# Reordering the DMA transposes at the end of each phase, and spreading the loads of x, in a causal convolution followed by a multiplicative feed-forward layer

## The chip, the core and the metric

The kernel runs on one core of a Trainium2 chip. The metric is the device time of one execution in microseconds (us); the median of three runs of the kernel before is 564.67 us (563.21 to 564.77). A core has five engines with instruction streams of their own: TensorE (PE in the profile, with its weight loads as PEld), VectorE (DVE), ScalarE (ACT), GpSimd (POOL) and SyncE (SP). In this kernel SP does nothing but issue DMAs: every store, and every transpose that a DMA does. POOL issues the DMAs that convert float32 to bfloat16 on the way. "SPq" in a row is the issue of a DMA by SP, and such issues follow each other in program order.

## The reference

The input x has 8 sequences of 3904 tokens with 192 features. Each of 8 heads (24 features) has 7 taps; a softmax over the taps gives the weights of a causal convolution along the sequence. Its result goes through a gated product:

```python
w = softmax(weight)                              # 8 heads x 7 taps
out = np.einsum('hk,bskhg->bshg', w, x_unf)      # causal, 6 zero rows ahead of each sequence
a = x @ w1                                       # x: 31232 x 192, w1 and w2: 192 x 1024
b = x @ w2
h = a * b @ w3                                   # w3: 1024 x 1024
return h @ w_out                                 # w_out: 1024 x 192
```

There is no nonlinearity behind w3, so the kernel multiplies w3 and w_out once (`W_sb`, 1024 x 192) and computes (a*b) @ W_sb.

## The kernel before, in words

**Tiling.** The 31232 tokens are two halves of 15616 (`NS = 2`); both halves are worked on side by side. A half is cut into 31 rounds of 512 tokens (`CH`). For a round, `first_product` computes for 8 slices of 128 of the 1024 columns the products `pa` and `pb` on PE (six matmuls each), ACT copies `pa` to bfloat16 (`asb`), and DVE multiplies it by `pb` into `abT` (L495). `second_product` then multiplies `abT` by `W_sb` on PE (`ops`, 32 matmuls), ACT copies the result to `osb`, and SP stores it to the output. `pa`, `pb`, `ops` and the convolution's `cps` take turns in four tiles of PSUM, so a `pa` or `pb` can start only when ACT or DVE has read an older one.

**Phases.** The first three rounds are a prologue. After that the program is written out as phases 0 to 14. Phase 0 has no first product; phase p from 1 on has the first products of rounds 2p+1 and 2p+2, then one side convolution on DVE (phases 1 to 12), then four second products of two older rounds (`seconds`, n = 0 to 3), between which units of the convolution on PE are placed, and last the DMA transposes for later phases. The order of the lines is the order in which each engine, and SP's queue, gets its work.

**Two ways to convolve.** The first product needs the convolved x transposed, with features on the partitions.

- Most rounds go over PE. The windows of x (32 rows, 26 of them new) are loaded in blocks b (`x_jobs`, into `xb`, six buffers, one or two parts per block), multiplied by a band matrix in units of some heads (`convolve`, `conv`, 18 units in blocks 4 to 9; `places` says after which second product of which phase), copied to `convo` by ACT, and when a block's last unit is done, stored to a scratch tensor `rows` in DRAM by SP (`store`, L349 and L356). The rounds that the block completes are put on the list `due`. From `rows` a DMA transpose brings them to `xT` (`transposes`, L390: three DMAs a round). `xT` is a ring of four rounds. Block 4 completes rounds 5 and 6 (in phase 0), block 5 rounds 7 and 8 (phase 1), block 6 rounds 11 to 14 (phase 3), block 7 rounds 17 to 20 (phase 6), block 8 rounds 23 to 26 (phase 9), block 9 rounds 29 and 30 (phase 11).
- The rounds of phases 4, 7, 10 and 13 (`SIDE`) go over DVE. Three times each, once for every 64 features, x is copied by two DMAs of POOL to a scratch tensor in bfloat16 (`side_cast`, into `rows_c`), transposed by two DMAs of SP (`side_transpose`, L427, into `raw`, two buffers) and convolved on DVE by seven instructions or more (`side_conv`, L437 and L444, from `raw` over `acc` into `side`). The cast of a task is issued in phase p, its transpose at the end of phase p, and its convolution on DVE behind the first products of phase p+1.

**POOL.** In a phase with casts or loads to issue (`jobs`), POOL copies two elements of a freshly written `abT` (`pace`, L682) at set points of the first products (`points`: round of the phase and slice), and behind each copy issues an equal share of the DMAs. The copy only holds POOL back until DVE has got there. `zero_rows` are the windows that start a sequence; POOL clears six rows of them (L675).

The end of a phase, before the change:

```python
        while due:
            transposes(due.pop(0))
        if p + 1 in tasks:
            side_transpose(*tasks[p + 1])
```

Of the kernel before, what the change touches and what calls it, by code (L numbers as in the profile page):

```python
# [16 lines left out]
def kernel(  # L17
# [10 lines left out]
    nc = tc.nc  # L28
# [6 lines left out]
    PAD = K - 1  # L35
# [70 lines left out]
    def shape_of(b):  # L106
        n = SIZES[b] // 4
        m = n // (1 if b < 3 else 2)
        return n, m, n // m
# [4 lines left out]
    xb_of, zero_rows = {}, {}  # L114

    def group(r, e):
        return slice((2 * r + e) * C, (2 * r + e) * C + C)
# [13 lines left out]
    def x_jobs(b, part):  # L131
        js = parts_of(b)[part]
        n, m, E = shape_of(b)
        tiles = xb_of.setdefault(b, {})

        def alloc():
            xb = work.tile([128, XN], BF16, tag="xb", bufs=6, name="xb")
            xb = xb[:, 0:len(js) * m * D].rearrange("p (w d) -> p w d", d=D)
            for j in js:
                tiles[j] = (xb, (j - js[0]) * m)  # L140
                for e in range(E):
                    for u in range(m):
                        i = FIRST[b] + j * n + u * E + e
                        if tok(i) % S == 0 and i:
                            zero_rows.setdefault(b, []).extend(
                                (xb, group(r, e).start, tiles[j][1] + u) for r in range(NS))

        def job(first, r, e, s, t, w):
            def run():
                if first:  # L150
                    alloc()
                nc.gpsimd.dma_start(  # L152
                    out=tiles[js[0]][0][group(r, e), s:s + w, :],
                    in_=bass.AP(tensor=x.tensor, offset=(r * TS + t - PAD) * D,
                                ap=[[D, C], [E * ST * D, w], [1, D]]))
            return run

        todo = [(r, e, s, t, w) for e in range(E) for s, t, w in runs_of(b, js, e)
                for r in range(NS)]
        return [job(i == 0, *a) for i, a in enumerate(todo)]  # L160
# [12 lines left out]
    for r in range(NS):  # L173
        p = group(r, 0).start
# [98 lines left out]
    p = group(1, 0).start  # L273
# [112 lines left out]
    def transposes(R, first=0):  # L386
        t0, t1 = max(R * CH, first), min((R + 1) * CH, TS)
        a = ring_of[R] * CH % RING + t0 - R * CH
        for k in range(NP):
            nc.sync.dma_start_transpose(  # L390
                out=xT[k][:, a:a + t1 - t0], in_=rows[t0:t1, k * 128:(k + 1) * 128])
# [17 lines left out]
    def side_span(p):  # L409
        return (2 * p + 1) * CH, (2 * p + 3) * CH  # L410

    def side_cast(p, k):
        t0, t1 = side_span(p)

        def job(r):
            def run():
                nc.gpsimd.dma_start(  # L417
                    out=rows_c[t0 - HALO:t1, k, r * Q:r * Q + Q],
                    in_=x_rows[r * TS + t0 - HALO:r * TS + t1, k * Q:k * Q + Q])
            return run  # L420
        return [job(r) for r in range(NS)]

    def side_transpose(p, k):
        t0, t1 = side_span(p)
        raw_of[p, k] = stage.tile([128, HALO + 2 * CH], BF16, tag="w3T", bufs=2, name="raw")
        for lo, hi in ((t0 - HALO, t0 + CH), (t0 + CH, t1)):
            nc.sync.dma_start_transpose(  # L427
                out=raw_of[p, k][:, HALO + lo - t0:HALO + hi - t0], in_=rows_c[lo:hi, k, :])
# [42 lines left out]
    def first_product(R, between=None):  # L471
        N = width(R)
        ab = work.tile([128, JT, NS, CH], BF16, tag="abT", bufs=LAG + 1, name="abT")
        abT_of[R] = ab
        per = CH // N if CH % N == 0 else 1
        for f0 in range(0, JT, per):
            pq = []
            for i in range(2):
                p = banks("pa" if i == 0 else "pb")
                pq.append(p)  # L480
                for f in range(per):
                    ft = f0 + f
                    for k in range(NP):
                        for r in range(NS):
                            rs = slice(Q * r, Q * r + Q)
                            nc.tensor.matmul(  # L486
                                p[:, r, f * N:f * N + N],
                                w_of(i, k, r)[rs, ft * 128:(ft + 1) * 128],
                                operand(R, k, rs),
                                start=(k == 0), stop=(k == NP - 1))  # L490
            pa, pb = pq
            asb = work.tile([128, NS, CH], BF16, tag="asb", bufs=3, name="asb")
            nc.scalar.copy(out=asb[:, :, 0:per * N], in_=pa[:, :, 0:per * N])  # L493
            if per == 1:
                nc.vector.tensor_tensor(out=ab[:, f0, :, 0:N], in0=asb[:, :, 0:N],  # L495
                                        in1=pb[:, :, 0:N], op=ALU.mult)
            else:
                i0, i1 = (t.rearrange("p r (f n) -> p r f n", f=per) for t in (asb, pb))
                nc.vector.tensor_tensor(
                    out=ab[:, f0:f0 + per, :, 0:N].rearrange("p f r n -> p r f n"),  # L500
                    in0=i0, in1=i1, op=ALU.mult)
            if between and f0 in between:
                between[f0]()
# [110 lines left out]
    def later_loads():  # L614
# [6 lines left out]
        for f in side_cast(SIDE[0], 0):  # L621
# [24 lines left out]
    units = [(b, h, n) for b in range(4, NB)  # L646
             for n in [max(v for v in (2, 4) if v * shape_of(b)[1] * G <= CH)]
             for h in range(0, H, n)]
    places = {0: (0, 1), 1: (0, 2), 2: (0, 2), 3: (0, 2), 4: (0,), 5: (0,), 6: (0, 2), 7: (0,),
              8: (0,), 9: (0, 2), 10: (0,), 11: (0,)}  # L650
    assert sum(map(len, places.values())) == len(units)
    tasks = {q - NP + k: (q, k) for q in SIDE for k in range(NP)}
    jobs = {p: side_cast(*tasks[p + 1]) for p in range(1, len(phases)) if p + 1 in tasks}
    for p, b, part in ((1, 6, 0), (1, 6, 1), (2, 7, 0), (3, 7, 1), (5, 8, 0), (6, 8, 1), (8, 9, 0)):
        jobs[p] = jobs.get(p, []) + x_jobs(b, part)
    points = ((0, 1), (0, 4), (0, 7), (1, 2), (1, 5))
    sent = [LAG + 3]
    due = []

    def convolve(p):  # L660
        b, h, n = units.pop(0)
        conv(b, h * G, n * G, (V, A) if p not in tasks else (A, A))
        if h + n == H:
            store(b)
            while sent[0] < len(conv_rounds) and \
                    min((conv_rounds[sent[0]] + 1) * CH, TS) <= spans[b - 3][1]:
                due.append(conv_rounds[sent[0]])
                sent[0] += 1
# [1 line left out]
    pace = const.tile([1, 2], BF16)  # L670
    done = 0
    for p, rounds in enumerate(phases):
        for b in {u[0] for u in units[:3]}:
            for xb, p0, w in zero_rows.pop(b, []):
                nc.gpsimd.memset(xb[p0:p0 + PAD, w, :], 0.0)  # L675
        if p == 1:
            P(out=wC[Q:128], in_=wC[0:Q])
        todo = jobs.pop(p, [])

        def issue(R, ft, n):  # L680
            def run():
                P(out=pace, in_=abT_of[R][0:1, ft, 1, 0:2])  # L682
                for _ in range(min(n, len(todo))):
                    todo.pop(0)()
            return run

        each = -(-len(todo) // len(points))
        for j, R in enumerate(rounds):
            first_product(R, {ft: issue(R, ft, each) for a, ft in points if a == j and todo})
        assert not todo  # L690
        if p in tasks:
            side_conv(*tasks[p])
        last = NR if p == len(phases) - 1 else done + 2
        seconds = [(R, r) for R in range(done, last) for r in range(NS)]
        done = last
        for n, (R, r) in enumerate(seconds):
            (last_product if (R, r) == (NR - 1, NS - 1) else second_product)(R, r)
            if n in places.get(p, ()):
                convolve(p)
        while due:  # L700
            transposes(due.pop(0))
        if p + 1 in tasks:
            side_transpose(*tasks[p + 1])
    assert not units and not due and not jobs and done == NR and sent[0] == len(conv_rounds)


# [28 lines left out]
```

## Time and profile before

| | |
|---|---|
| median of the runs | 564.67 us |
| time of the profiled execution | 564.64 us |
| its span, from the first instruction to the last | 562.9 us |
| PE, DVE, ACT busy | 93%, 74%, 60% of the span |
| TensorE clock granted, mean | 0.964 of full speed |
| DVE idle ahead of L437 | 54.1 us in 4 pieces |
| DMA transposes into xT, into raw | 60, 24 |

Engine rows of a timeline give the start and the length in us, the engine, the line, the operation and what is written and read, with the number of instructions merged; a bracket at the end has the idle time before it and what ended that. Rows of the chain of work that ended last give start, length and what the program's end was waiting on at that time. Busy PE says little by itself, since matmuls are pipelined; what counts is how far apart the phases start on PE.

### The profile page before, as it was taken

How to read it: one execution, taken by the hardware profiler on the slowest of the kernel's cores; microseconds unless marked ns; L12 is line 12 of the kernel's file. 1: busy time of each engine (PE TensorE's matmuls, PEld its weight loads, DVE VectorE, ACT ScalarE, POOL GpSimd, SP SyncE). 2: the span in 40 equal slices, each digit the busy share in tenths (PEclk: the TensorE clock that was granted, in tenths of full speed). 3: DMA queues.
4: the chain of work that ended last, by engine and by line, in shares of the span. 5: the costliest groups of instructions: out<-in, count | busy, mean ns of one | idle time of the engine just before them, and what ended most of it. 6: DMA issues, size and time to landing. Idle time of an engine off the chain costs nothing.

```text
span 562.9 us, 14352 instructions
## 1 busy us (share of the span) xinstructions
PE 520.9 (93%) x6148; PEld 339.8 (60%) x6148; DVE 417.2 (74%) x410; ACT 340.4 (60%) x392; POOL 88.1 (16%) x180
## 2 busy tenths in 40 slices
PE   8999997589999994999999949999995999999997
PEld 4457746446657581484765715748573475675877
DVE  7797392579797928898978199798855897989280
ACT  6775574446776743657676526576753556657462
POOL 9773060020130100203110013010100100000000
PEclk9999999779999997899999969999999899999999
DMA  9999399994664944928476645432946325030304
GB/s 143 153 162 181 60 189 167 199 141 70 122 74 117 161 90 140 90 74 116 64 145 136 156 64 58 132 20 89 164 88 168 20 53 148 20 113 1 113 2 141
DMA packets 149745, 61.19 MB, mean 109 GB/s; under 512 B 102709, under 2 KB 149681, under 8 KB 149681
## 3 DMA queue, kind: packets, MB, share of 16 engines
q1 hardware_dynamic: 88992, 42.83, 31.6%
q0 software_dynamic: 60672, 17.44, 31.1%
q8 instruction: 48, 0.79, 0.6%
q14 instruction: 17, 0.13, 0.1%
q10 hardware_dynamic: 16, 0.00, 0.0%
HBM read 35.16 MB, written 34.85 MB: 124 GB/s over the span
## 4 chain that ended last, share of the span: by engine, by line
PE 83%; DVE 6%; DMA 5%; SPq 2%; issue 2%; ACT 1%; POOL 1%; DVEq 0%; POOLq 0%; ACTq 0%
PE ops L511 27%; PE pb L486 27%; PE pa L486 26%; DVE acc L444 4%; DMA raw<-rows_c 3%; PE cps L318 2%; DMA xb<-in_x_dram 1%; DVE abT L495 1%; PE wps L579 1%; SPq L427 1%; SPq L390 1%; DMA wn<-in_moe_w_dram 1%; DVE acc L437 1%; ACT asb L493 0%; POOL xb L152 0%
## 5 line engine op out<-in xcount | busy, mean ns | idle before, releaser
L495 DVE TENSOR_TENSOR abT<-asb,pb 128x1024 bf16<-128x1024 bf16 x240 | 292.0, 1221 | 66.5 <-ACT asb L493 49.2
L493 ACT CAST asb<-pa 128x1024 bf16<-128x1024 f32 x244 | 247.1, 1013 | 105.8 <-PE pa L486 87.7
L486 PEld LDWEIGHTS <-ws 64*128 64x128 bf16 x1488 | 133.0, 95 | 107.7 <-issue 39.9
L486 PEld LDWEIGHTS <-wn 64*128 64x128 bf16 x1488 | 140.3, 95 | 86.9 <-issue 7.3
L486 PE MATMUL pb<-xT,wn 64*128 64x512 bf16 (+1 forms) x552 | 151.8, 381 | 23.7 <-DVE abT L495 23.7
L511 PE MATMUL ops<-W_sb,abT 128*128 128x192 bf16 x1936 | 167.1, 248 | 0.0
L511 PEld LDWEIGHTS <-abT 128*128 128x128 bf16 x1936 | 159.5, 98 | 8.7 <-issue 8.1
L486 PE MATMUL pa<-xT,wn 64*128 64x512 bf16 (+1 forms) x552 | 150.0, 380 | 9.3 <-DVE abT L495 8.2
L486 PE MATMUL pa<-xT,ws 64*128 64x512 bf16 (+1 forms) x552 | 150.1, 381 | 0.0
L486 PE MATMUL pb<-xT,ws 64*128 64x512 bf16 (+1 forms) x552 | 148.9, 382 | 0.0
L516 ACT COPY osb<-ops 128x768 f32<-128x768 f32 (+1 forms) x61 | 48.5, 794 | 100.5 <-PE ops L511 100.5
L444 DVE SCALAR_TENSOR_TENSOR acc<-raw,wC,acc 128x1024 f32<-128x1024 bf16 (+10 forms) x90 | 78.7, 925 | 1.3
L682 POOL COPY pace<-abT 1x2 bf16<-1x2 bf16 x41 | 7.1, 174 | 316.4 <-DVE abT L495 316.3
L486 PE MATMUL pb<-side,wn 64*128 64x512 bf16 x192 | 52.0, 376 | 0.0
L486 PE MATMUL pa<-side,wn 64*128 64x512 bf16 x192 | 51.8, 376 | 0.0
L486 PE MATMUL pa<-side,ws 64*128 64x512 bf16 x192 | 51.7, 376 | 0.0
L486 PE MATMUL pb<-side,ws 64*128 64x512 bf16 x192 | 51.4, 376 | 0.0
L437 DVE TENSOR_SCALAR acc<-raw,wC 128x1024 f32<-128x1024 bf16 x12 | 9.0, 750 | 54.1 <-DMA raw<-rows_c 54.1
L327 ACT CAST convo<-cps 128x640 bf16<-128x640 f32 (+4 forms) x70 | 39.1, 635 | 5.5 <-PE cps L318 5.4
L152 POOL DMA_DIRECT2D xb<-in_x_dram x64 | 40.5, 638 | 7.9 <-issue 3.7
L417 POOL DMA_DIRECT2D rows_c<-in_x_dram x24 | 18.7, 779 | 6.9 <-issue 6.2
L318 PE MATMUL cps<-xb,Aband 32*32 32x120 bf16 (+2 forms) x1088 | 13.7, 233 | 4.1 <-issue 3.1
(65 smaller groups left out, 106.7 us busy)
## 6 DMA issues: line engine op xcount, KB each, us to landing
out_dram<-osb SPq DMA_DIRECT2D x58, 384.0 KB
xb<-in_x_dram POOLq DMA_DIRECT2D x28, 240.0 KB, 7.2
rows_c<-in_x_dram POOLq DMA_DIRECT2D x24, 130.0 KB, 4.1
rows<-convo SPq DMA_DIRECT2D x9, 240.0 KB
xb<-in_x_dram POOLq DMA_DIRECT2D x8, 228.0 KB, 6.5
rows<-convo SPq DMA_DIRECT2D x9, 150.0 KB
xb<-in_x_dram POOLq DMA_DIRECT2D x8, 168.0 KB, 4.9
rows<-convo SPq DMA_DIRECT2D x9, 120.0 KB
```

Of the source, the lines that this page charges most:

```text
L152: nc.gpsimd.dma_start(out=tiles[js[0]][0][group(r, e), s:s + w, :], in_=bass.AP(tensor=x.tensor, offset=(r * TS + t - PAD) * D, ap=[[D, C] ...
L318: nc.tensor.matmul(o.rearrange("p (w g) -> p w g", g=wd)[:, :, c - c0:c1 - c0], Aband[group(r, e), h, :], xb[group(r, e), s:s + m, c:c1], ...
L327: f(out=convo[:, e::E, k, :, lo:lo + c] .rearrange("p w r g -> p r w g"), in_=src[:, :, :, o:o + c])
L417: nc.gpsimd.dma_start(out=rows_c[t0 - HALO:t1, k, r * Q:r * Q + Q], in_=x_rows[r * TS + t0 - HALO:r * TS + t1, k * Q:k * Q + Q])
L437: nc.vector.tensor_scalar(out=acc, in0=raw[:, HALO - 1:HALO - 1 + t1 - t0], scalar1=wC[:, k, K - 2:K - 1], scalar2=None, op0=ALU.mult)
L444: nc.vector.scalar_tensor_tensor(out=out, in0=raw[:, HALO + lo - t0 - d:HALO + hi - t0 - d], scalar=wC[:, k, K - 1 - d:K - d], in1=acc[:, ...
L486: nc.tensor.matmul(p[:, r, f * N:f * N + N], w_of(i, k, r)[rs, ft * 128:(ft + 1) * 128], operand(R, k, rs), start=(k == 0), stop=(k == NP ...
L493: nc.scalar.copy(out=asb[:, :, 0:per * N], in_=pa[:, :, 0:per * N])
L495: nc.vector.tensor_tensor(out=ab[:, f0, :, 0:N], in0=asb[:, :, 0:N], in1=pb[:, :, 0:N], op=ALU.mult)
L511: nc.tensor.matmul(ops[:, g // 2, (g % 2) * D:(g % 2) * D + D], ab[:, jt, r, g * 128:(g + 1) * 128], W_sb[:, jt, :], start=(jt == 0), stop ...
L516: nc.scalar.copy(out=osb.rearrange("p (a g) d -> p a (g d)", g=2), in_=ops[:, 0:ng // 2, 0:2 * D])
L682: P(out=pace, in_=abT_of[R][0:1, ft, 1, 0:2])
```

## The change

Five things are edited in the loop over the phases:

1. At the end of a phase the transposes of `raw` are issued first, and behind them those of `xT` for at most two rounds of `due`; further rounds stay on the list until the end of the next phase.
2. The loads of a block of x that has two parts go to two successive phases: block 6 to phases 1 and 2, block 7 to 3 and 4, block 8 to 6 and 7; block 9 to phase 9.
3. There are six points per phase instead of five, at other slices.
4. The units of the convolution move: phase 2 has one instead of two, phase 3 three instead of two, phases 4 and 7 none instead of one, phases 5 and 8 two instead of one.
5. The clearing of `zero_rows` stands behind the first products of a phase instead of at its start.

```diff
-    places = {0: (0, 1), 1: (0, 2), 2: (0, 2), 3: (0, 2), 4: (0,), 5: (0,), 6: (0, 2), 7: (0,),
-              8: (0,), 9: (0, 2), 10: (0,), 11: (0,)}
+    places = {0: (0, 1), 1: (0, 2), 2: (2,), 3: (0, 1, 2), 5: (0, 2), 6: (0, 2),
+              8: (0, 2), 9: (0, 2), 10: (0,), 11: (0,)}
...
-    for p, b, part in ((1, 6, 0), (1, 6, 1), (2, 7, 0), (3, 7, 1), (5, 8, 0), (6, 8, 1), (8, 9, 0)):
+    for p, b, part in ((1, 6, 0), (2, 6, 1), (3, 7, 0), (4, 7, 1), (6, 8, 0), (7, 8, 1), (9, 9, 0)):
         jobs[p] = jobs.get(p, []) + x_jobs(b, part)
-    points = ((0, 1), (0, 4), (0, 7), (1, 2), (1, 5))
+    points = ((0, 1), (0, 3), (0, 5), (0, 7), (1, 2), (1, 4))
...
     for p, rounds in enumerate(phases):
-        for b in {u[0] for u in units[:3]}:
-            for xb, p0, w in zero_rows.pop(b, []):
-                nc.gpsimd.memset(xb[p0:p0 + PAD, w, :], 0.0)
...
         for j, R in enumerate(rounds):
             first_product(R, {ft: issue(R, ft, each) for a, ft in points if a == j and todo})
         assert not todo
+        for b in {u[0] for u in units[:3]}:
+            for xb, p0, w in zero_rows.pop(b, []):
+                nc.gpsimd.memset(xb[p0:p0 + PAD, w, :], 0.0)
         if p in tasks:
             side_conv(*tasks[p])
...
-        while due:
-            transposes(due.pop(0))
         if p + 1 in tasks:
             side_transpose(*tasks[p + 1])
+        for R in due[:2]:
+            transposes(R)
+        del due[:2]
```

## The prediction, made before the change was run

> **What bounds the kernel now.** I read the page first.
>
> ```profile
> PEclk9999999779999997899999969999999899999999
> ...
> PE 83%; DVE 6%; DMA 5%; SPq 2%; issue 2%; ACT 1%; POOL 1%; DVEq 0%; POOLq 0%; ACTq 0%
> ...
> L437 DVE TENSOR_SCALAR acc<-raw,wC 128x1024 f32<-128x1024 bf16 x12 | 9.0, 750 | 54.1 <-DMA raw<-rows_c 54.1
> ```
>
> PE carries 83% of the chain that ended last, so time can be won only where PE stands. The granted clock dips four times, and the first instruction of a side convolution, on DVE, waits 54.1 us for the transposes into `raw`. The waits say how often:
>
> ```profile
> DVE acc L437 <- DMA raw<-rows_c: 54.1, 4, 16.5
> ```
>
> Four of the twelve tasks wait. Next, PE's timeline gave me the start of each phase, its first `pa`; that of phase 4:
>
> ```profile
> 178.56 0.39 PE L486 MATMUL pa<-side,wn 64*128 64x512 bf16 x1
> ```
>
> With the twelve starts and that of phase 13 as borders, busy times by stretch give one row per phase, 1 to 12 (length, then PE, PEld, DVE, ACT and POOL busy, granted clock, DMA share, GB/s):
>
> ```profile
> 65.23:103.09 37.86, 34.77 (x449) 23.08 (x449) 19.54 (x16) 23.15 (x28) 9.04 (x18) 0.95 1.18 151
> 103.09:146.14 43.05, 35.37 (x387) 22.03 (x386) 36.20 (x30) 22.93 (x26) 4.80 (x9) 0.88 0.75 137
> 146.14:178.56 32.42, 32.42 (x387) 21.09 (x386) 27.92 (x23) 22.93 (x26) 6.22 (x13) 1.00 0.63 97
> 178.56:210.51 31.95, 31.95 (x353) 20.80 (x353) 19.54 (x16) 21.07 (x22) 2.08 (x5) 1.00 0.67 121
> 210.51:253.46 42.95, 35.24 (x354) 22.05 (x354) 36.55 (x42) 21.20 (x24) 4.76 (x9) 0.88 0.56 103
> 253.46:285.88 32.42, 32.42 (x387) 20.97 (x386) 28.18 (x29) 22.92 (x26) 6.22 (x13) 1.00 0.61 101
> 285.88:317.83 31.95, 31.95 (x353) 20.82 (x353) 19.54 (x16) 21.07 (x22) 2.09 (x5) 1.00 0.69 124
> 317.83:360.79 42.96, 33.75 (x353) 21.68 (x353) 36.55 (x42) 21.20 (x24) 7.98 (x17) 0.88 0.51 98
> 360.79:393.21 32.42, 32.42 (x386) 20.97 (x386) 28.18 (x29) 22.92 (x26) 2.08 (x5) 1.00 0.34 71
> 393.21:425.45 32.24, 32.24 (x386) 21.38 (x386) 19.54 (x16) 20.98 (x24) 2.05 (x5) 1.00 0.72 123
> 425.45:467.50 42.05, 33.90 (x386) 22.19 (x386) 36.11 (x30) 20.88 (x24) 2.05 (x5) 0.92 0.39 85
> 467.50:499.00 31.50, 31.50 (x323) 20.76 (x322) 27.92 (x23) 19.35 (x20) 0.00 (x0) 1.00 0.32 91
> ```
>
> In phases 1, 4, 7 and 10 DVE is busy 19.54 us and does 16 instructions: the side convolution is missing. It runs in the phase after, which has 36.2 to 36.6 us of DVE work and takes 42 to 43 us. Elsewhere PE is busy for the whole phase: 31.50 us without a convolution unit (phase 12), 31.95 with one, 32.42 with two, so a unit of 32 matmuls costs 0.47, and one of 64 (block 9, phase 10) 0.74.
>
> Why `raw` is late, SP in phase 4:
>
> ```profile
> 178.11 10.54 SPq L356 DMA_DIRECT2D rows<-convo  x8
> ...
> 191.30 17.58 SPq L390 DMA_TRANSPOSE xT<-rows  x12
> 209.05 2.45 SPq L427 DMA_TRANSPOSE raw<-rows_c  x2
> ```
>
> and DVE beside it:
>
> ```profile
> 180.46 20.64 DVE L495 TENSOR_TENSOR abT<-asb,pb 128x1024 bf16<-128x1024 bf16 x16 [3.19 <-ACT asb L493]
> 213.11 0.76 DVE L437 TENSOR_SCALAR acc<-raw,wC 128x1024 f32<-128x1024 bf16 x1 [12.00 <-DMA raw<-rows_c]
> ...
> 221.84 4.61 DVE L495 TENSOR_TENSOR abT<-asb,pb 128x1024 bf16<-128x1024 bf16 x4
> ```
>
> Block 6 is finished in phase 3, and its twelve transposes to `xT` hold SP for 17.6 us ahead of `raw`. DVE is ready at 180.46+20.64 = 201.10 and starts at 213.11; the `abT` that PE needs to go on follow at 221.84.
>
> **The change, part by part.** *Raw first.* The issue of `raw` moves from 209.05 to 191.30. Its two issues take 2.45 us in a quiet queue. In phase 1, when x is being loaded, a transpose takes 13.74/6 = 2.29 us:
>
> ```profile
> 78.91 1.61 SPq L521 DMA_DIRECT2D out_dram<-osb  x2
> 83.69 13.74 SPq L390 DMA_TRANSPOSE xT<-rows  x6
> ```
>
> The landing behind the issue that the chain shows is 2.74 us at best and 5.00 us at worst:
>
> ```profile
> 98.99 5.00 DMA raw<-rows_c
> ...
> 210.25 2.74 DMA raw<-rows_c
> ```
>
> So `raw` lands between 191.30+2.45+2.74 = 196.5 and 191.30+4.58+5.00 = 200.9, ahead of 201.10 at both ends. There is slack as well: the convolution takes 221.84-213.11 = 8.73 us, and the next phase's first `abT` comes 180.46-178.56 = 1.90 us behind that phase's start, at 212.41; a start by 203.7 costs nothing. Phases 7 and 10 repeat phase 4. In phase 1 SP is free at 80.52, `raw` lands at 85.7 to 90.1, and by the same count (phase 2 starting at 98.2) 91.4 is early enough. I take the whole excess as won in all four places:
>
> - phase 2: 43.05-32.42 = 10.63
> - phase 5: 42.95-31.95 = 11.00
> - phase 8: 42.96-31.95 = 11.01
> - phase 11: 42.05-32.24 = 9.81
>
> Together 42.45 us. The halved clock after a standstill is in these differences, so it isn't counted again:
>
> ```profile
> 115.64 1.28 PE pa L486 x6
> ...
> 121.67 0.65 PE pa L486 x6
> ```
>
> Six matmuls take 1.28 us after the stall and 0.65 once the clock is back. The Trainium skill's "TensorE: Matmul & The Clock Gate" (Part 1, The HAM clock gate) puts the halving behind an idle window of about 3.4 us; the trace agrees, with stalls of 7 us and more ahead of each dip.
>
> *What is late next: xT.* The first two rounds of a block are issued behind `raw`, from 193.75 at 17.58/12 = 1.47 us each: six end at 202.5 and land by 207.5, and phase 5 starts at 210.51 with the first of them alone. The next two come a phase later, at the end of phase 4's list, and are read in phase 6. In phase 1, at the loaded price, round 5 is issued by 85.1+3x2.29 = 92.0 and lands by 97.0 for 98.2; round 6 has ten more. Cost zero; without this cover each us late is a us of PE.
>
> *The loads of x.* Phase 1 keeps the first half of block 6, four large loads, and two casts. The second half goes to phase 2, where its unit now runs behind the third second product. With two per point (four large, two small, two casts over six points) the last large load leaves at slice 5, about 11 us into the phase, and its landing was 4.2 us in a quiet stretch and 18.4 in phase 1:
>
> ```profile
> xb<-in_x_dram POOLq DMA_DIRECT2D x1, 228.0 KB, 18.4
> xb<-in_x_dram POOLq DMA_DIRECT2D x2, 240.0 KB, 4.2
> ```
>
> So it lands 15 to 29 us in, and is read at 20.64+3x(31.50-20.64)/4 = 28.8. Only the bad end misses, by a fraction; I take zero. Blocks 7, 8 and 9 have a phase or more. One more `pace` copy a phase falls to a POOL that is busy 9.04 us at most in a phase; behind the copy stand these loads only. The cleared rows belong to block 5 in phase 0, which has no first products: no cost.
>
> *The units.* Phases 2 and 3 exchange one, 4 gives one to 5, 7 one to 8: 18 units before and after, so the sum is zero. Three in a row in phase 3 fit: between two units PE has 2.71 for a second product and 0.47, and ACT's copies of one are 1.83 long with 0.80 for `osb`.
>
> ```profile
> 175.56 0.80 ACT L516 COPY osb<-ops 128x768 f32<-128x768 f32 x1 [1.84 <-PE ops L511]
> 176.26 1.83 ACT L327 CAST convo<-cps 128x960 bf16<-128x960 f32 x2
> ```
>
> *The pause in phase 1.* That phase is 37.86-31.50-2x0.74 = 4.88 us too long, with no late `raw` in it:
>
> ```profile
> 98.23 0.52 PE L318 MATMUL cps<-xb,Aband 32*32 32x120 bf16 x40 [3.09 <-issue]
> ```
>
> PE stops within a unit, with nothing that the profile names, and the clock then halves. The DMA share of that phase, 1.18, is the highest of all, and a packet of PE's instruction queue lies in this gap; I read it as instructions that came late through full DMA engines. The price is bounded by 0 (nothing changes) and 4.88 (all goes). With half the loads gone from the phase I take 4.88.
>
> Sum: 564.64-42.45-4.88 = 517.3 for the profiled execution, whose time is 0.03 below the median of the runs (564.67), so the median is forecast at 517.3 as well.
>
> **The rivals.**
>
> - *The pause stays* (522.2). For it: SP still puts the output, block 4's store and eight transposes into that phase. Against it: eight large loads become four. The Trainium skill's "DMA: Bandwidth & Descriptors" (Queues, rings and completion order) says that each engine goes round between its queues packet by packet. By that rule an instruction packet waits for a packet of each other queue however long the backlog is; halving the loads would change nothing, and the time would be 522.2. No run so far tells the two apart.
> - *Raw stays a little late in phases 4 and 7*, where four large loads now run beside it. At the loaded issue price and twice the worst landing it comes at 191.3+4.58+10.0 = 205.9, that is 2.2 us beyond 203.7 in two phases: 521.7. At the far end phases 5 and 8 keep all of their excess: 517.3+22.0 = 539.3. Against it: the bound above holds with the loaded prices.
> - *Slower*: the later `xT` rounds become the wait, at the starts of phases 5, 6, 8, 9, 11 and 12. To eat 47.3 us each of the six has to lose 7.9 us. The first round's third transpose, at 193.75+3x1.47+5.0 = 203.2 by my count, would have to land at 218.4, 15 us later, and so in every block. At 20 us late it is 517.3+6x12.7 = 593.5. No landing of a transpose in the chain above is over 5.00.
> - *Nothing changes*: `raw` is held by something else than the queue, say its cast, and only comes first in line: 564.6. Against it: SP goes from the last `xT` to `raw` at 209.05 within 0.2 us, without a wait.
>
> **How the numbers follow.** Forecast (pause gone, four waits gone, 517.3) 0.58; pause stays 0.21; `raw` late in part 0.13; slower 0.04; nothing 0.04. What a measurement can tell from no change is 0.3%, 1.7 us. The range goes down by the spread of the three runs (563.21 to 564.77, 1.6 us) and one such 1.7 to 514; up it takes in the pause and the two late phases at the small price, 522.2+4.4 = 526.6, and one more pause like that of phase 1, to 531. That leaves out the last two cases and the far end of the third, some 0.14. Faster 0.92, same 0.04, slower 0.04.
>
> **What would show it.** Right: no DVE idle time for `raw`; DVE busy near 28 us in every phase from 1 to 12; phases of 31.5 to 33 us; PE's clock at 1.00 from phase 2 on; on SP, L427 ahead of L390 and L390 in sixes. Wrong: DVE waiting for `raw` in phases 4 or 7; PE waiting for `xT` at a phase's start; PE pauses put to issue, in phase 1 or elsewhere; a unit of phase 2 waiting for `xb`.

## The result, and the profile after

The changed kernel takes 518.83 us (median of five runs, 517.43 to 520.15) against 564.67 us (563.21 to 565.35): a ratio of 0.9195 with a 95% interval of 0.9168 to 0.9222. The forecast was 517.3, in a range of 514 to 531. The profiled execution took 519.86 us with a span of 518.2, so 44.7 us of the span are gone, where the prediction's sum said 47.3.

From the page of the changed kernel, the rows that answer to those shown of before:

```profile
span 518.2 us, 14372 instructions
...
PEclk9999999999999999999999999999999999999999
...
PE 95%; DVE 1%; ACT 1%; DMA 1%; POOL 1%; issue 1%; DVEq 0%; ACTq 0%; POOLq 0%
...
L437 DVE TENSOR_SCALAR acc<-raw,wC 128x1024 f32<-128x1024 bf16 x12 | 9.0, 749 | 10.7 <-DMA xT<-rows 5.4
```

The four dips of the clock are gone, PE has 95% of the chain instead of 83%, and DVE's idle time ahead of L437 fell from 54.1 to 10.7 us. It is not zero, and that is where the missing 2.6 us begin. The row puts half of the 10.7 us, the wait in phase 1, down to a transpose to `xT`; but L437 reads `raw` and not `xT`, and in another execution of the changed kernel the wait in phase 1 is put down to `raw`, so I count it as a wait for `raw`. Busy times by stretch, again with the starts of the phases as borders (length, PE, PEld, DVE, ACT and POOL busy, clock, DMA share, GB/s); the rows are those of phases 1 to 5, 8 and 11:

```profile
64.81:98.41 33.60, 33.11 (x449) 21.62 (x449) 25.07 (x21) 23.24 (x28) 5.51 (x13) 1.00 1.06 160
98.41:131.32 32.91, 32.13 (x353) 21.59 (x354) 30.59 (x26) 21.08 (x22) 6.07 (x12) 1.00 1.05 163
131.32:164.20 32.88, 32.88 (x418) 21.18 (x418) 27.92 (x23) 24.78 (x30) 5.38 (x12) 1.00 0.63 96
164.20:195.69 31.49, 31.49 (x321) 20.64 (x321) 25.35 (x26) 19.35 (x20) 6.07 (x12) 1.00 1.16 163
195.69:229.01 33.32, 32.59 (x385) 21.72 (x386) 30.84 (x33) 22.93 (x26) 2.27 (x6) 1.00 0.49 99
...
292.92:325.44 32.52, 32.52 (x386) 21.70 (x386) 30.14 (x32) 22.92 (x26) 2.27 (x6) 1.00 0.54 101
...
390.21:422.45 32.24, 32.24 (x386) 21.28 (x386) 27.91 (x23) 20.89 (x24) 2.23 (x6) 1.00 0.53 101
```

Every phase is now within 1 us of what its units of the convolution ask for. By the prices of the prediction (31.50 us, 0.47 per unit, 0.74 per large one) phase 1 is 0.62 over, phase 2 0.94, phase 5 0.88 and phase 8 0.08, together 2.5 of the missing 2.6 us; phases 3 and 4, with three units and none, are at their sums within 0.03. The units that changed places cost nothing.

SP and DVE around the end of phase 3, the place that the prediction worked out:

```profile
163.75 11.42 SPq L356 DMA_DIRECT2D rows<-convo  x8
175.21 1.59 SPq L349 DMA_DIRECT2D rows<-convo  x1
176.91 0.73 SPq L521 DMA_DIRECT2D out_dram<-osb  x1
177.82 3.95 SPq L427 DMA_TRANSPOSE raw<-rows_c  x2
181.87 10.04 SPq L390 DMA_TRANSPOSE xT<-rows  x6
```

```profile
166.10 20.65 DVE L495 TENSOR_TENSOR abT<-asb,pb 128x1024 bf16<-128x1024 bf16 x16 [3.64 <-ACT asb L493]
189.84 0.76 DVE L437 TENSOR_SCALAR acc<-raw,wC 128x1024 f32<-128x1024 bf16 x1 [3.09 <-DMA raw<-rows_c]
```

`raw` follows the block's store, as predicted, and the transposes to `xT` come in sixes behind it. But DVE is ready at 186.75 and still waits 3.09 us: the two issues take 3.95 us, and DVE starts 8.07 us behind their end (in the kernel before it was 1.6 to 3.9 us, wherever DVE waited). The wait is 5.38 us in phase 1 and 2.29 us in phase 7; in phase 10, which has no load of x beside it, there is none. Of the pause in phase 1 something is left, too:

```profile
95.21 0.53 PE L318 MATMUL cps<-xb,Aband 32*32 32x120 bf16 x40 [0.49 <-issue]
```

### The profile page after: what moved, and what is told of

Its sections match the earlier page's. It is cut to its first block, busy times and chain, and to the rows that moved or that the text cites. A ratio compares the mean times of both kernels' runs of the same rounds, so it can differ in the third digit from the quotient of the medians.

```text
span 518.2 us, 14372 instructions
## 1 busy us (share of the span) xinstructions
PE 510.5 (99%) x6148; PEld 336.4 (65%) x6148; DVE 417.7 (81%) x410; ACT 340.5 (66%) x392; POOL 90.5 (17%) x191
## 4 chain that ended last, share of the span: by engine, by line
PE 95%; DVE 1%; ACT 1%; DMA 1%; POOL 1%; issue 1%; DVEq 0%; ACTq 0%; POOLq 0%
PE ops L511 32%; PE pb L486 30%; PE pa L486 30%; PE cps L318 2%; PE wps L579 1%; DMA wn<-in_moe_w_dram 1%; DVE abT L495 1%; ACT asb L493 1%; ACT convo L327 0%; POOL xb L152 0%; PE ops L532 0%; PE tps L365 0%; DVE xT L372 0%; POOL wn L220 0%; POOL wn L221 0%
## 5 line engine op out<-in xcount | busy, mean ns | idle before, releaser
L486 PEld LDWEIGHTS <-wn 64*128 64x128 bf16 x1488 | 137.7, 94 | 84.0 <-issue 2.2
L486 PEld LDWEIGHTS <-ws 64*128 64x128 bf16 x1488 | 130.3, 94 | 72.6 <-issue 2.5
L486 PE MATMUL pb<-xT,wn 64*128 64x512 bf16 (+1 forms) x552 | 147.5, 371 | 1.5 <-DVE abT L495 1.5
L486 PE MATMUL pa<-xT,wn 64*128 64x512 bf16 (+1 forms) x552 | 145.6, 372 | 0.3 <-DVE xT L372 0.2
L486 PE MATMUL pa<-xT,ws 64*128 64x512 bf16 (+1 forms) x552 | 145.6, 372 | 0.0
L486 PE MATMUL pb<-xT,ws 64*128 64x512 bf16 (+1 forms) x552 | 143.2, 371 | 0.0
L679 POOL COPY pace<-abT 1x2 bf16<-1x2 bf16 x52 | 9.2, 176 | 263.8 <-DVE abT L495 263.7
L417 POOL DMA_DIRECT2D rows_c<-in_x_dram x24 | 18.7, 782 | 6.6 <-issue 6.5
L437 DVE TENSOR_SCALAR acc<-raw,wC 128x1024 f32<-128x1024 bf16 x12 | 9.0, 749 | 10.7 <-DMA xT<-rows 5.4
L444 DVE SCALAR_TENSOR_TENSOR side<-raw,wC,acc 128x1024 bf16<-128x1024 bf16 x12 | 15.4, 1285 | 0.4
```

What stands on the lines that cost most here:

```text
L417: nc.gpsimd.dma_start(out=rows_c[t0 - HALO:t1, k, r * Q:r * Q + Q], in_=x_rows[r * TS + t0 - HALO:r * TS + t1, k * Q:k * Q + Q])
L437: nc.vector.tensor_scalar(out=acc, in0=raw[:, HALO - 1:HALO - 1 + t1 - t0], scalar1=wC[:, k, K - 2:K - 1], scalar2=None, op0=ALU.mult)
L444: nc.vector.scalar_tensor_tensor(out=out, in0=raw[:, HALO + lo - t0 - d:HALO + hi - t0 - d], scalar=wC[:, k, K - 1 - d:K - d], in1=acc[:, ...
L486: nc.tensor.matmul(p[:, r, f * N:f * N + N], w_of(i, k, r)[rs, ft * 128:(ft + 1) * 128], operand(R, k, rs), start=(k == 0), stop=(k == NP ...
```

## The experiments

The kernel before ran beside each group of experiments, on the same chip as they did; its medians there were 563.25, 563.28, 564.59 (one run) and 559.46 us. Ratios are each to the kernel before of the same group.

### The order alone

```diff
-        while due:
-            transposes(due.pop(0))
         if p + 1 in tasks:
             side_transpose(*tasks[p + 1])
+        for R in due[:2]:
+            transposes(R)
+        del due[:2]
```

> The order at the end of a phase alone (raw first, xT two rounds a phase); loads, points and units as before the change. Theory: the order carries the gain of the four waits. Phases 2, 5, 8 and 11 fall to 32 to 33 us, DVE's wait for raw to under 6 us in all, and phases 4 and 7, which have no large load now, show no wait at all (the changed kernel had 3.09 and 2.29 us there). Phase 1 has its eight large loads again. If full DMA engines make the pause of PE's instructions there, it is back at about 3 us with a halved clock behind it, and phase 1 takes 36 to 38 us: in all 521 to 525. Rival, by which an instruction packet waits a packet of each other queue and no backlog matters: the pause stays at the 0.49 us of the changed kernel, in all 516 to 518. Rival, the gain is that of the loads: 555 or more.

Measured: 522.54 us, ratio 0.9291 (0.9237 to 0.9345). Phases 1, 2, 4, 5, 8 and 11 of this kernel, by stretch:

```profile
64.38:102.31 37.93, 34.47 (x450) 22.75 (x450) 25.68 (x22) 23.14 (x28) 9.03 (x18) 0.96 1.18 150
102.31:135.02 32.71, 32.59 (x385) 21.73 (x385) 29.95 (x25) 22.93 (x26) 4.80 (x9) 1.00 1.20 181
...
167.44:199.40 31.96, 31.96 (x354) 20.88 (x354) 28.18 (x29) 21.07 (x22) 2.09 (x5) 1.00 0.69 137
199.40:231.35 31.95, 31.95 (x353) 20.95 (x352) 28.18 (x29) 21.20 (x24) 4.77 (x9) 1.00 0.84 123
...
295.73:327.69 31.96, 31.96 (x354) 20.90 (x354) 28.17 (x29) 21.20 (x24) 7.99 (x17) 1.00 0.82 117
392.35:424.58 32.23, 32.23 (x385) 21.18 (x385) 27.91 (x23) 20.88 (x24) 2.05 (x5) 1.00 0.54 101
```

The order carries the gain: phases 2 and 5 fall from 43.05 and 42.95 to 32.71 and 31.95, and phase 4 does its own side convolution (28.18 us of DVE work instead of 19.54). Without large loads in phases 4 and 7 DVE waits for `raw` in one place only, phase 1, where the eight loads are (9.05 us). And phase 1 is as long as before the change:

```profile
97.79 0.64 PE L318 MATMUL cps<-xb,Aband 32*32 32x120 bf16 x40 [3.46 <-issue]
```

So the new order does nothing for the pause: it goes with the other edits. The section on the pause singles out the loads among them.

### Is it the raw transposes' place, or the halving of the list?

Raw first, but all due rounds behind it at once:

```diff
-        while due:
-            transposes(due.pop(0))
         if p + 1 in tasks:
             side_transpose(*tasks[p + 1])
+        while due:
+            transposes(due.pop(0))
```

> Only the two statements at the end of a phase exchanged: raw first, and all due rounds of xT behind it at once; loads, points and units as before the change. Theory: xT has a phase to spare, so it doesn't matter whether six or twelve follow raw: same as the kernel with the order edits alone within 0.3%. Rival: twelve in a row hold SP for 17.6 us behind raw, past the end of the next phase's first second products, and output stores that come late hold osb buffers and ACT: phases 4, 7 and 10 longer by 1 to 3 us, 4 to 8 us in all.

Measured: 523.88 us (521.76 to 525.32), ratio 0.9311 (0.9252 to 0.937); the profiled executions of this kernel and of the one before it have the same span, 520.0 us. In phase 4:

```profile
182.99 17.50 SPq L390 DMA_TRANSPOSE xT<-rows  x12
200.57 3.16 SPq L521 DMA_DIRECT2D out_dram<-osb  x4
```

Twelve transposes behind `raw` hold SP for 17.50 us and delay the first output stores of the next phase, which nobody waits for. With the loads where they were, two rounds a phase are no part of the gain that these runs can tell.

Two rounds a phase, but ahead of raw:

```diff
-        while due:
-            transposes(due.pop(0))
+        for R in due[:2]:
+            transposes(R)
+        del due[:2]
         if p + 1 in tasks:
             side_transpose(*tasks[p + 1])
```

> Two rounds of xT at most per phase, but still ahead of raw; loads, points and units as before the change. Theory: in phases 4, 7 and 10 raw then stands behind six instead of twelve and lands at 191.3+8.8+2.45+2.74 to 5.00 = 205.3 to 207.5 on the time scale of the kernel before, 1.6 to 3.8 us beyond the 203.7 that cost nothing, so phases 5, 8 and 11 lose 1.6 to 3.8 us each instead of 9.8 to 11.0; phase 2 keeps its 10.6 and phase 1 its pause, since six were due there anyway: 538 to 545. Rival, any transposes ahead of raw cost the whole wait: 560 to 565. Rival, half the queue is as good as none: 530 to 533.

Measured: 534.22 us (533.26 to 536.35), ratio 0.9492 (0.9426 to 0.9558), below the 538 to 545 of the theory and just above the 530 to 533 of the last rival. The profiled execution, 536.35 us, is the slowest of its four. Phases 1, 2, 5 and 8, and SP at the end of phase 3:

```profile
65.52:102.16 36.64, 33.12 (x450) 21.61 (x450) 19.54 (x16) 23.23 (x28) 9.04 (x18) 1.00 1.15 152
102.16:147.42 45.26, 35.38 (x386) 22.08 (x386) 36.20 (x30) 22.92 (x26) 4.79 (x9) 0.89 0.81 136
211.80:243.99 32.19, 32.12 (x353) 21.47 (x353) 30.26 (x32) 21.20 (x24) 4.76 (x9) 1.00 0.78 122
308.36:342.30 33.94, 32.31 (x355) 21.51 (x354) 31.97 (x36) 21.20 (x24) 7.99 (x17) 1.00 0.67 111
```

```profile
192.58 8.72 SPq L390 DMA_TRANSPOSE xT<-rows  x6
201.46 2.44 SPq L427 DMA_TRANSPOSE raw<-rows_c  x2
```

DVE waits 3.05, 4.79 and 3.10 us in phases 4, 7 and 10, and the phases behind them lose 0.24, 1.99 and 0.03 us. That is the slack of the prediction, measured: a wait of about 3 us is free, one of 4.8 costs 2.0. The theory's size was off because it took waits of 1.6 to 3.8 us beyond the slack, and two of the three ended within 0.5 us of it. Phase 2, where six were due before too, keeps its loss (45.26 us here).

### The loads alone

All other edits, with the old order at the end of a phase (the diff is against the changed kernel):

```diff
+        while due:
+            transposes(due.pop(0))
         if p + 1 in tasks:
             side_transpose(*tasks[p + 1])
-        for R in due[:2]:
-            transposes(R)
-        del due[:2]
```

> All other edits (loads, points, units, place of the clearing) without the new order: xT for all due rounds ahead of raw. Theory: the four waits stay, and those of phases 4 and 7 grow by the loads that now run beside the transposes; the pause in phase 1 shrinks to about 0.5 us: 4 us less there, 2 to 6 us more in phases 5 and 8: 558 to 567. Rival, the loads carry a good part of the gain: 550 or less.

Measured: 559.92 us, ratio 0.9969 (0.9934 to 1.0004): its gain over the kernel before can't be told from none. Phases 1, 2 and 5, and its waits for `raw`:

```profile
64.36:97.38 33.02, 33.02 (x450) 21.67 (x450) 21.22 (x18) 23.14 (x28) 5.49 (x13) 1.00 1.06 166
97.38:135.70 38.32, 33.60 (x355) 21.70 (x354) 34.50 (x29) 21.07 (x22) 6.04 (x12) 0.96 0.84 135
200.07:245.98 45.91, 35.71 (x386) 22.27 (x386) 36.54 (x42) 22.92 (x26) 2.26 (x6) 0.85 0.35 81
```

```profile
DVE acc L437 <- DMA raw<-rows_c: 48.8, 4, 14.9
```

Inside, it is a sum of both signs. Phase 1 is 4.84 us shorter than before (37.86), with no pause; phase 2 is 4.73 shorter (0.47 of it is the unit that moved to phase 3), because `raw` comes less late with fewer loads beside it: SP's six transposes ahead of it take 9.88 us instead of 13.74, and DVE waits 8.74 us instead of 16.53. Phases 5 and 8 are 2.96 and 3.09 longer (0.47 of each is the unit that moved there), because the loads now run beside the transposes of phases 4 and 7: the twelve of phase 4 take 19.45 us instead of 17.58, and DVE waits 14.04 and 14.89 us instead of 12.00 and 13.50. The expectation had left out the gain in phase 2. The same loads that free phase 1 cost the two later places something, in the changed kernel too.

### What is left: raw beside the new loads

The changed kernel was run twice more, each time beside variants of itself, first here:

> The changed kernel itself, beside the next three on the same chip: 517 to 520.

Measured: 518.65 us (517.56 to 522.63), ratio 0.9227 (0.9194 to 0.926).

The transposes of `raw` ahead of the phase's second products, block store and output stores:

```diff
         if p in tasks:
             side_conv(*tasks[p])
+        if p + 1 in tasks:
+            side_transpose(*tasks[p + 1])
         last = NR if p == len(phases) - 1 else done + 2
...
-        if p + 1 in tasks:
-            side_transpose(*tasks[p + 1])
         for R in due[:2]:
```

> The changed kernel with the transposes of raw for the next phase issued behind the first products, ahead of the second products, the block's store and the output stores of the phase. In the changed kernel raw still lands 5.4, 3.1 and 2.3 us after DVE is ready in phases 1, 4 and 7, and phases 2, 5 and 8 are 0.9, 0.9 and 0.1 us over the sum of their parts. Theory: raw is late there because the store and the new x loads go ahead of it; issued some 10 us earlier it lands in time, DVE never waits, and the three phases lose their excess: 1.9 us less than the changed kernel, 516 to 518. Rival: raw then waits for its cast at the head of SP's queue and holds the stores: no gain or slower.

Measured: 517.23 us (517.09 to 518.02), ratio 0.9195 (0.9168 to 0.9222). DVE waits for `raw` nowhere. Phases 1, 2, 5 and 8:

```profile
64.70:98.62 33.92, 33.12 (x450) 21.66 (x450) 27.91 (x23) 23.15 (x28) 5.49 (x13) 1.00 1.01 147
98.62:130.57 31.95, 31.95 (x353) 20.86 (x352) 27.92 (x23) 21.07 (x22) 6.05 (x12) 1.00 1.30 184
194.95:227.36 32.41, 32.41 (x385) 21.00 (x385) 28.18 (x29) 22.92 (x26) 2.26 (x6) 1.00 0.50 100
291.28:323.69 32.41, 32.41 (x385) 20.96 (x385) 28.18 (x29) 22.92 (x26) 2.26 (x6) 1.00 0.60 102
```

Phases 2, 5 and 8 have lost their excess; phase 1 has a pause of 0.81 us in this execution.

The loads of blocks 7, 8 and 9 one phase earlier:

```diff
-    for p, b, part in ((1, 6, 0), (2, 6, 1), (3, 7, 0), (4, 7, 1), (6, 8, 0), (7, 8, 1), (9, 9, 0)):
+    for p, b, part in ((1, 6, 0), (2, 6, 1), (2, 7, 0), (3, 7, 1), (5, 8, 0), (6, 8, 1), (8, 9, 0)):
```

> The changed kernel with the loads of blocks 7, 8 and 9 one phase earlier (phases 2 and 3, 5 and 6, 8), so that phases 4 and 7 have no large load; block 6 stays spread over phases 1 and 2. Theory: the waits of 3.1 and 2.3 us in phases 4 and 7 come from those loads and go; phases 5 and 8 fall to 32.42, 1.0 us less than the changed kernel in all: 516.5 to 519. Rival: the waits come from the third unit in phase 3 or the later store: no difference.

Measured: 517.42 us (516.96 to 520.91), ratio 0.9209 (0.9176 to 0.9241). DVE waits in phase 1 only (4.09 us), and phases 5 and 8 take 32.41 us each:

```profile
194.02:226.43 32.41, 32.41 (x385) 20.95 (x385) 28.18 (x29) 22.92 (x26) 5.31 (x12) 1.00 0.86 125
290.35:322.76 32.41, 32.41 (x385) 20.95 (x385) 28.18 (x29) 22.92 (x26) 8.17 (x18) 1.00 0.84 120
```

So the waits of phases 4 and 7 came from the loads that the change had put there, not from the third unit in phase 3, which is still in this kernel.

Both, the last two edits together:

> Both of the last two. Theory: either removes the waits of phases 4 and 7, so the two together give what the early raw gives alone, 516 to 518, and the least DMA traffic beside raw. Rival: the two add up, 515 to 516.5.

Measured: 517.82 us (516.79 to 518.76), ratio 0.9203 (0.9174 to 0.9232). The three variants can't be told from each other.

The pair was run once more:

> The changed kernel once more, as the partner of the next: 517.5 to 520.

> The early raw once more, since its lead over the changed kernel (517.23 against 518.65) was of the size of what five rounds can tell. If the lead is that of the waits for raw, whose cost in phases 2, 5 and 8 changed from run to run between 0.6 and 1.9 us, it is again 0.5 to 2 us, and DVE has no wait for raw. Rival, chance: between -0.5 and 0.5.

Measured: 517.55 us (516.94 to 518.65) and 516.85 us (516.69 to 517.1), ratios 0.9242 (0.921 to 0.9274) and 0.9229 (0.9201 to 0.9258). The early raw leads in both pairs, by 1.4 and 0.7 us, and DVE again has no wait for `raw`, but the intervals overlap each time. What the profiles do show is that the changed kernel's excess in phases 2, 5 and 8 differs from one execution to the next (0.94, 0.88 and 0.08 us; 0, 0 and 0.7; 0.6, 0 and 0), and that of the early raw stays at zero. In the second pair five of the six runs of the changed kernel lie above all six of the early raw. It is the version I would keep, for a lead of 0.1 to 0.3% that the intervals don't settle.

### The pause

Twelve large loads in phase 1 instead of four, otherwise the changed kernel:

```diff
-    for p, b, part in ((1, 6, 0), (2, 6, 1), (3, 7, 0), (4, 7, 1), (6, 8, 0), (7, 8, 1), (9, 9, 0)):
+    for p, b, part in ((1, 6, 0), (1, 6, 1), (1, 7, 0), (4, 7, 1), (6, 8, 0), (7, 8, 1), (9, 9, 0)):
```

> The changed kernel with twelve large loads of x in phase 1 instead of four (both halves of block 6 and the first half of block 7). Theory, that the pause of PE in phase 1 comes from full DMA engines: it was 0.49 us with four loads and 3.08 to 3.52 us with eight, and the instruction packet of that gap left at 92.6 us with four and at 94.4 to 96.3 with eight; with twelve the pause is 3 us or more, and phase 1 takes 37 us or more. Rival, a packet by packet turn, by which only the presence of a second busy queue counts: between 0.5 and 3.5 us, no more than with eight. DVE's wait for raw in phase 1 grows beyond the 9 us that eight loads gave.

Measured: 523.82 us in one run (564.59 before). Phase 1 takes 38.25 us, and DVE's wait for `raw` there is 10.69 us. The pause is longer than with eight loads, but by 0.12 us only, which doesn't decide between the theory and the rival. Its row:

```profile
98.03 0.63 PE L318 MATMUL cps<-xb,Aband 32*32 32x120 bf16 x40 [3.64 <-issue]
```

And none, on top of the early raw:

```diff
-    places = {0: (0, 1), 1: (0, 2), 2: (2,), 3: (0, 1, 2), 5: (0, 2), 6: (0, 2),
+    places = {0: (0, 1), 1: (0, 2), 3: (0, 1, 2, 3), 5: (0, 2), 6: (0, 2),
...
-    for p, b, part in ((1, 6, 0), (2, 6, 1), (3, 7, 0), (4, 7, 1), (6, 8, 0), (7, 8, 1), (9, 9, 0)):
+    for p, b, part in ((2, 6, 0), (2, 6, 1), (3, 7, 0), (4, 7, 1), (6, 8, 0), (7, 8, 1), (9, 9, 0)):
```

> The kernel with the early raw, with no load of x in phase 1 (both halves of block 6 in phase 2, and their four units in phase 3); the two casts stay. Theory: with GpSimd's queue empty from about 80 us on, the instruction packet leaves at 86 to 89 us, when PE gets to its chunk, as it does in quiet phases, and the pause is 0: phase 1 takes 33.0 us. Rival, that the pause is a matter of SP's own stores and transposes: 0.5 us or more remain.

Measured: 519.38 us in one run. Phase 1 has no pause (33.02 us), though the packet starts at 90.3 us and not at 86 to 89. Phase 4 takes 32.81 us instead of 31.50, so this is no better kernel. The fourth unit of phase 3 stands at the very end of that phase, ACT copies it (1.83 us) ahead of the first `asb` of phase 4, and PE waits 0.49 us for the `abT` that follows; where the rest of the 1.3 us goes is open.

All kernels in one table. The third column is the start of the packet of PE's instruction queue that ends the pause, counted from the start of phase 1, or, where there is no pause, of the packet in the same place:

| large loads of x in phase 1 | profiled executions | packet starts, us into the phase | pause, us |
|---|---|---|---|
| 0 | 1 | 24.6 | 0 |
| 4 | 8 | 26.9 to 27.9 | 0 to 0.81 |
| 8 | 4 (before among them) | 29.7 to 30.8 | 3.08 to 3.52 |
| 12 | 1 | 31.1 | 3.64 |

That the packet is what PE waits for is read from the times: in all seven kernels with a pause, PE goes on 1.2 to 1.7 us behind the end of this packet. The kernel without loads has the early raw; the two runs of the early raw with four loads have the packet at 27.9 and 26.9. The more loads, the later the packet, which decides for the loads and against a pause of SP's own making. It doesn't settle how. From 0 to 8 loads each four add about 3 us, the next four only some 0.7: that fits a backlog (the last four loads are issued too late to stand ahead of the packet) and it fits a turn-taking that has reached its limit. These runs don't tell the two apart.

## Why the prediction was right, and where its sum was off

- **Raw first, 42.45 us.** Right in kind and nearly in size: the order alone brought phases 2, 5, 8 and 11 down by 10.34, 11.00, 11.00 and 9.82 us, 42.2 in all. In the changed kernel 1.9 of it is given back in phases 2, 5 and 8.
- **"`raw` lands between 196.5 and 200.9 ... ahead of 201.10 at both ends"** is the step that failed: DVE waits 5.4, 3.1 and 2.3 us in phases 1, 4 and 7. The bound took 5.00 us, the longest landing in the trace of before, as the worst. That landing begins with the second issue (98.99), not with the end of both (100.44), so the sum was more generous than its rows; it was too short all the same, because the 5.00 was read where the last loads were just ending (POOL's DMA queue took 18.7% of the DMA engines' time from 97.55 to 104.00; in the changed kernel it took 52.9% from 177 to 190). The bound's upper end lies 22.3 us into phase 4; DVE started 25.6 us in. SP got to `raw` 0.9 us later in the phase than before, the landing took 8.07 us instead of 5.00, and the issue, 3.95 instead of 4.58, gave 0.6 back. The rival "`raw` stays a little late in phases 4 and 7" so came true beside the forecast, but at 0.9 and 0.1 us instead of 2.2 each: it had taken a landing of 10.0 us. The slack of 2.6 us behind DVE's readiness, which the prediction had worked out, took the rest. The excess in phase 2 is of the same kind: the 91.4 that it called early enough became 92.74. Two of the prediction's signs of being wrong so did show, DVE waiting for `raw` in phases 4 and 7 and a pause put to issue; with the wait in phase 1 they cost 2.5 us in all.
- **The pause, 4.88 us.** Taken whole, and 4.3 us of it came: 0.49 us is left in the profiled execution. Both halves of the reasoning hold: the loads make it, and half the loads nearly end it. How much half the loads would leave was not worked out, though, so that the size came out is in part luck. The Trainium skill's rule of a turn per packet ("DMA: Bandwidth & Descriptors", Queues, rings and completion order), from which the prediction had derived that the pause would stay, did not decide here: halving the loads moved the packet by about 3 us. The kernel with twelve loads fits a limit, as such a rule would have it, but doesn't show one.
- **The clock.** The prediction saw stalls of 7 us and more ahead of the dips. Its own pause of 3.09 us halved the clock as well, for 3.41 us; the last section has the rows.
- **Costs put at zero.** The units' new places, the later `xT`, the extra point and the place of the clearing cost nothing that shows, taken together: in the profiled execution no PE wait for `xT` or `xb` appears in phases 1 to 14, and phases 3, 4, 6 and 7 are at their sums. The second half of block 6 was in time in phase 2.
- **Slower, or no change**: the mechanism named for slower (`xT` late at a phase's start) appears nowhere, not even with twelve transposes behind `raw`.

## What to carry to other kernels

A queue that issues in order is a schedule: when an engine waits for a transfer, look first at what stands ahead of it in the issuing queue, and sort by when each transfer is needed, not by when it became possible. Busy times by stretch, cut at the starts of a repeated phase, give the gain before the change is made: the phases without the wait are the price list for those with it. And a landing time read in one place is no bound once the same change moves other traffic beside it; what saved the forecast was the slack behind the wait, which should be worked out every time.

## What the runs showed of the hardware that was not expected

- The two DMA transposes of `raw` took SP 2.4 to 3.0 us to issue in phases 4, 7 and 10 with no large load beside them, 3.2 to 5.2 us beside four large converting loads in the changed kernel and 6.9 to 7.5 beside eight or twelve. Where DVE waited, it could start 1.6 to 3.9 us behind the end of the two issues in the kernel before, 5.5 to 8.1 us beside the four loads, and 8.3 to 9.7 beside eight or twelve.
- A pause of PE of the same length costs differently from run to run. With 3.46 us, the kernel with the order alone had a granted clock of 0.96 in phase 1 and 37.93 us; with 3.52 us, the kernel with two rounds ahead of raw kept a clock of 1.00 and took 36.64 us. The traces suggest why. Between the start and the end of a kernel the clock was halved for 3.41, 6.83, 10.24 or 13.65 us at a time, whole multiples of 3.41 us, so it seems to be set window by window. In the kernel before, PE was busy for 1.14 us of the window that holds most of the pause (the first number behind the length), and the clock of the next window was 0.50:

```profile
95.96:99.37 3.41, 1.14 (x49) 1.00 1.52 106
99.37:102.78 3.41, 3.41 (x24) 0.50 1.64 169
```

In the kernel with two rounds ahead of raw the pause lies across two windows:

```profile
93.84:97.25 3.41, 1.59 (x41) 1.00 1.78 173
97.25:100.66 3.41, 1.71 (x55) 1.00 1.29 113
```

PE was busy for 1.14 us of its window or less in the four pauses of phase 1 that halved the clock (1.14, 1.01, 0.27 and 0.04) and for 1.59 or more where the clock stayed. The Trainium skill's "TensorE: Matmul & The Clock Gate" (Part 1, The HAM clock gate) says that the window of about 3.4 us runs freely, which agrees with this; where it puts the halving behind an idle window, these runs differ, since pauses of 3.08 and 3.09 us, shorter than the window, halved the clock too. Gaps of 0.5 to 1.5 us left it at 1.00.
- The profile's page has a queue of kind "instruction" with 48 packets and 0.79 MB; that it carries PE's instructions is read from PE going on behind its packets. With up to eight loads of about 240 KB in the phase, a packet started some 3 us later per four loads. With four, PE paused 0 to 0.81 us.
